# Layer norm's inverse root from one table set, the first loads in another order, and new task places in an attention and MLP kernel

## The chip, the cores and the metric

The kernel runs on one core of one Trainium2 chip. The time is device microseconds of that core, from the first to the last instruction of one execution with what lies around it; lower is better. Five engines work side by side, each through its own list of instructions in order: TensorE (PE; its weight loads stand as PEld), VectorE (DVE), ScalarE (ACT), GpSimd (POOL) and SyncE (SP), which here only issues DMAs. An instruction that must wait for another engine or a DMA holds up everything behind it in its own list.

## The reference

```python
q_rot, k_rot = rotate(q), rotate(k)                 # rotary embedding; 4 batches, 8 heads, 576 tokens, 64 wide
scores = matmul(q_rot, k_rot^T) / sqrt(64)
attn = exp(scores - max); attn /= attn.sum(-1) + 1e-9
x = matmul(attn, v)                                 # heads side by side: 2304 tokens x 512
mu = mean(x); var = mean((x - mu) ** 2)             # over the 512 features
xn = (x - mu) / sqrt(var + 1e-6) * g_ln
out = x + maximum(xn @ w_ch1, 0) @ w_ch2            # 512 -> 2048 -> 512
```

All tensors are float32. The two MLP weight matrices arrive as 64-bit floats and are decoded on the chip.

## The kernel before

**Tiling.** Attention goes over 16 pairs of heads. A pair has nine units of 128 query rows by 576 keys. For a unit TensorE makes the scores (L486; L499 for the tail unit), DVE takes the negated maximum of a row (L513), ACT the exponential with its sum (L520). The weights are then turned, on TensorE with copies by ACT (L580 to L604) or by DVE (L568), and multiplied with v (L654 or L680). DVE scales the result into the tile `xt` (L692 to L706).

**Blocks.** The 2304 tokens are five blocks, one of 512 and four of 448. Each passes a layer norm: a mean by a product with a constant matrix (L766), centring on DVE (L790), squares on ACT (L796), the variance by products (L780) into four strips of PSUM, the standard deviation by ACT's Sqrt (L808), its reciprocal on DVE (L811), a product that spreads it back over the partitions (L816), and the scaling by `g` (L825). The first block's MLP runs during attention (L1007). The other four run as two pairs of blocks in a scheme with seven products in place of eight (L1180), whose inputs are sums and differences of the normed blocks. These are written to DRAM as `hat` (L838) and read back (L1126). ACT rounds each input to a high part (L1088) and DVE or GpSimd subtracts it for the low part (L1095).

**Weights.** Each 512 KB piece of the weights is loaded as raw bits (L859), decoded by ACT, DVE and GpSimd (L868, L871, L874, L877, L880), split into a high and a low part (L893, L897), and kept in DRAM for the later blocks.

**Order.** Every step is a task with a function, the tasks that it needs, and the buffers that it takes and gives. The strings `PLACES` and `SIDES` hold each task's rank and, where a task may run on either of two engines, which one. A planner walks the tasks with assumed durations, and the order it finds is fixed on each engine. So a new string of ranks gives a new list on every engine.

**The start.** The first pair's keys are loaded in two halves of 288, the queries in 128 and 448. The first key half and the queries are issued by SP, the second key half by ACT. Rotating a half takes two products and a sum on DVE (L387), the last 448 query columns on GpSimd. The first scores need the first key half and the first 128 queries. TensorE multiplies an identity with itself 16 times meanwhile (`WARM`, L1310). One table set for ACT, with Exp, is loaded at the start (L358).

The names that matter below: `constants` and `constants3` (memsets, L351 to L364), `first_pair` (L366 on), `deviation`, `inverse` and `spread` inside `layer_norm` (L806 to L816), `pair_inputs` (L1126).

Of the kernel before, what the change touches and what calls it, by code (L numbers as in the profile page):

```python
# [64 lines left out]
WARM = 16  # L65
# [200 lines left out]
def rope_attention_then_ln_mlp(  # L266
# [477 lines left out]
    def layer_norm(n):  # L744
# [65 lines left out]
        def inverse():  # L810
            DVE.reciprocal(z["std"], z["std"])  # L811
# [597 lines left out]
```

## Time and profile before

| what | us |
|---|---|
| median of 3 runs (670.94 to 672.25) | 671.86 |
| the profiled execution | 673.72 |
| its span, first to last instruction | 671.8 |
| TensorE busy | 630.5 (94%) |
| VectorE busy | 552.2 (82%) |
| ScalarE busy | 358.5 (53%) |
| GpSimd busy | 297.6 (44%) |

The chain of work that ended last lies on TensorE for 64% of the span, on VectorE for 16%, on DMA for 8% and on ScalarE for 6%. A busy share is a mean over stages with different limits, so the rows below are read stage by stage. Line numbers are those of the kernel before. In the changed kernel L387 is L390, L486 is L489, L808 is L811 and L812, L811 is L817 to L819, L816 is L824, and lines from there on are 8 higher.

### The profile page before, as it was taken

The page shows a single profiled execution, that of the slowest core. Times are in us where ns is not written, and L with a number is a line of the kernel's source. Part 1 is how long each engine was busy: PE and PEld are TensorE (multiplying, and loading weights), DVE is VectorE, ACT ScalarE, POOL GpSimd, SP SyncE. Part 2 cuts the span into 40 slices and gives each one's busy share as a digit, 9 for nine tenths or more (in the row PEclk, how much of TensorE's full clock was granted, in tenths as well). Part 3 has the DMA queues.
Part 4 walks back from the last instruction along what each step waited for, and adds up shares of the span by engine and source line. Part 5 has one row for each costly group of instructions (what it writes and reads, how often), then busy time and mean ns, then how long its engine had stood idle before and what let it go on. Part 6 is the DMA issues. An engine that isn't in the chain of part 4 may idle for free.

```text
span 671.8 us, 13940 instructions
## 1 busy us (share of the span) xinstructions
PE 630.5 (94%) x5268; PEld 491.4 (73%) x5268; DVE 552.2 (82%) x887; ACT 358.5 (53%) x734; POOL 297.6 (44%) x223
## 2 busy tenths in 40 slices
PE   5899988999899999898898699899999999999997
PEld 4555647766675757666576587799889999999997
DVE  4998788589899989899955789978789786857876
ACT  2898877467678876688644246342343143223230
POOL 2636663454566558477510254853324212404042
PEclk7999998999999999999999899999999999999999
DMA  8477574668669889886877688778876887766666
GB/s 273 125 243 238 182 200 151 202 232 239 218 219 266 277 278 293 263 270 233 272 236 214 203 257 285 244 271 268 293 254 210 266 267 219 218 221 211 212 208 201
DMA packets 89283, 158.42 MB, mean 236 GB/s; under 512 B 11776, under 2 KB 57344, under 8 KB 88704
## 3 DMA queue, kind: packets, MB, share of 16 engines
q1 hardware_dynamic: 88080, 156.67, 73.2%
q10 hardware_dynamic: 1136, 0.85, 0.4%
q8 instruction: 42, 0.69, 0.4%
q14 instruction: 25, 0.20, 0.1%
HBM read 117.57 MB, written 39.92 MB: 234 GB/s over the span
## 4 chain that ended last, share of the span: by engine, by line
PE 64%; DVE 16%; DMA 8%; ACT 6%; issue 4%; POOL 1%; SPq 0%; ACTq 0%; DVEq 0%; POOLq 0%
PE n L1180 34%; PE sc L1007 9%; PE sc L486 6%; PE sc L654 5%; PE sc L680 4%; DVE mx L513 3%; PE sc L580 3%; ACT pt L520 2%; DMA w<-in_w2p 2%; DMA w<-s 2%; DVE pt L568 2%; DMA s<-ws 1%; ACT pt L598 1%; PE sc L499 1%; DVE tmp L1218 1%
## 5 line engine op out<-in xcount | busy, mean ns | idle before, releaser
L1180 PE MATMUL n<-x,w 128*128 128x448 f32 x672 | 143.0, 371 | 7.9 <-ACT x L1088 2.6
L1180 PEld LDWEIGHTS n<-x,w 128*128 128x128 f32 x672 | 126.5, 189 | 22.9 <-DVE x L1095 3.4
L520 ACT ACTIVATE pt<-sc,mx 128x576 f32<-128x576 f32 x144 | 105.7, 739 | 54.9 <-DVE mx L513 54.2
L1180 PE MATMUL n<-o,w 128*128 128x448 f32 x576 | 120.8, 368 | 1.9 <-DVE acc L1276 1.3
L513 DVE TENSOR_REDUCE mx<-sc 128x1 f32<-128x576 f32 x144 | 102.8, 747 | 19.5 <-PE sc L486 16.0
L1180 PEld LDWEIGHTS n<-o,w 128*128 128x128 f32 x576 | 107.7, 188 | 13.1 <-DVE acc L1276 1.7
L1088 ACT ACTIVATE o<-tmp 128x448 fp32r<-128x448 f32 x96 | 53.3, 574 | 103.1 <-PE n L1180 39.8
L486 PE MATMUL sc<-x 64*128 64x288 f32 x512 | 93.5, 442 | 8.4 <-DVE x L387 6.4
L486 PEld LDWEIGHTS sc<-x 64*128 64x128 f32 x512 | 53.1, 192 | 35.9 <-ACT pt L520 8.4
L1095 POOL TENSOR_TENSOR o<-tmp,o 128x448 fp32r<-128x448 f32 x33 | 43.1, 1319 | 81.8 <-ACT o L1088 71.5
L877 POOL TENSOR_TENSOR fw<-fw,w 128x512 int32<-128x512 int32 x32 | 43.3, 1356 | 55.7 <-ACT w L871 27.0
L1252 DVE TENSOR_TENSOR xt<-xt,n 128x448 f32<-128x448 f32 x80 | 47.8, 613 | 9.7 <-PE n L1180 8.5
L654 PE MATMUL sc<-pt,v 128*64 128x512 f32 (+2 forms) x324 | 50.5, 417 | 0.9 <-ACT pt L520 0.9
L680 PE MATMUL sc<-pt,v 32*64 32x160 f32 (+1 forms) x2016 | 43.7, 301 | 5.6 <-issue 2.1
L654 PEld LDWEIGHTS sc<-pt,v 128*64 128x64 f32 (+1 forms) x324 | 22.4, 142 | 33.7 <-issue 29.7
L680 PEld LDWEIGHTS sc<-pt,v 32*64 32x64 f32 x2016 | 36.7, 135 | 12.6 <-issue 6.6
L568 DVE STREAM_TRANSPOSE pt<-pt 128x1152 f32<-128x1152 f32 (+1 forms) x35 | 43.1, 1241 | 3.3 <-ACT pt L520 3.3
L1007 PE MATMUL sc<-xh,w 128*128 128x512 f32 x128 | 44.7, 410 | 0.7 <-ACT pt L520 0.7
L1007 PE MATMUL sc<-hh,w 128*128 128x512 f32 x128 | 44.3, 405 | 0.4 <-issue 0.4
L580 PE MATMUL sc<-ident,pt 128*128 128x128 f32 x288 | 38.1, 278 | 5.9 <-ACT pt L520 4.6
L1218 DVE SCALAR_TENSOR_TENSOR tmp<-tmp 128x448 f32<-128x448 f32 x48 | 40.6, 854 | 3.3 <-ACT tmp L1225 2.9
L580 PEld LDWEIGHTS sc<-ident,pt 128*128 128x128 f32 x288 | 31.3, 141 | 13.2 <-ACT pt L520 9.1
(129 smaller groups left out, 1062.2 us busy)
## 6 DMA issues: line engine op xcount, KB each, us to landing
w<-s SPq DMA_DIRECT2D x64, 512.0 KB
w<-v SPq DMA_DIRECT2D x96, 256.0 KB
s<-ws SPq DMA_DIRECT2D x24, 512.0 KB
v<-in_vp SPq DMA_DIRECT2D x37, 320.0 KB
x<-in_qk SPq DMA_DIRECT2D x30, 288.0 KB
xs<-in_qk SPq DMA_DIRECT2D x30, 288.0 KB
w<-in_w1p SPq DMA_DIRECT2D x16, 512.0 KB
w<-in_w2p SPq DMA_DIRECT2D x16, 512.0 KB
```

Of the source, the lines that this page charges most:

```text
L486: PE.matmul(ps[:, a, :HS], lhsT=q[r, c * P : (c + 1) * P], rhs=k[r, KEYS[a]], start=True, stop=True)
L513: DVE.tensor_reduce(out=mx, in_=st["ps", i, n][:, :, :HS], axis=AX.XY, op=ALU.max, negate=True)
L520: ACT.activation(out=halves(p), in_=st.pop(("ps", i, n))[:, :, :HS], func=AF.Exp, bias=st.pop(("mx", i, n)), scale=1.0, accum_out=total)
L568: DVE.transpose(p, p)
L580: PE.transpose(two[:, j, k * P : (k + 1) * P], p[:, at : at + P], ident)
L654: yield lambda o=o, x=x: PE.matmul(o, lhsT=w, rhs=x, start=start, stop=stop)
L680: PE.matmul(tiles[a // 2][j * D : (j + 1) * D, a % 2, x0 : x0 + (u1 - u0) * BLK], lhsT=v[r, of, k * P + j * D : k * P + (j + 1) * D], rhs= ...
L1007: PE.matmul(ps, lhsT=wt, rhs=x, start=c + m == 0, stop=c + m == NC + 1)
L1088: ACT.activation(out=o[0], in_=x(), func=AF.Relu if relu else AF.Copy)
L1180: PE.matmul(ps, lhsT=wt, rhs=x, start=fresh and kc + z == 0, stop=kc + z == 3, skip_group_check=True)
L1218: return lambda: DVE.scalar_tensor_tensor(out=out(), in0=x(), scalar=0.0, in1=y(), op0=ALU.max, op1=ALU.subtract)
L1252: DVE.tensor_tensor(out=o, in0=o, in1=ps(which, h), op=ALU.add)
```

## The change

ACT's Sqrt and DVE's reciprocal become Ln, Exp with the factor -0.5, and one Newton step of three instructions on DVE that works in the variance's own PSUM strip. The table set that holds both Ln and Exp is loaded once at the start. In the first loads SP issues the cosines ahead of the keys, and each load is ranked behind the one before it. The constants' tasks have other assumed durations, the warm-up has 20 products, and all ranks and sides are new (a line of them is shown).

```diff
-WARM = 16
+WARM = 20
...
 PLACES = (
-    "AAANADAFAEAGACABAHARAVAXAUATAWAMAKAPAdAYAgAaAlAQAIAJASA1A9A)AbA4A#A,AZAcAeAoAnAqAkAvA0AzA2AuA5A7A6A!A+A/A>A<A@A=A]A}A~BBA3A$A8A(A%A.BHBOBMBS",
+    "AAAFAHABAEAGACADAIAPAOASAQATAXAUAVAWAeAYAhAZAnARAJAKANA8AqA*AaAzA&A,AbAdAiAkAjApAmAyA1A0A3AsA2A7A6A!A+A.A=A<A>A;A]BAA_BDA5A$A9A)A%A-BKBUBHBM",
...
         for o, i in second:
             ACT.dma_start(o, i)
+        ACT.preload_act_table_set("natural_log_exp_and_others")
         ACT.activation(out=first, in_=eps_ln, func=AF.Exp)
...
-        def dma(kb, pairs, prio=-90.0):
+        def dma(kb, pairs, prio=-90.0, behind=()):
...
+            if not pairs:
+                return add({"NONE": 6.2}, go, (), prio)
...
-        l1 = dma(288, keys(KEYS[0]))
-        l2 = dma(128, queries(head))
+        l1 = dma(288, keys(KEYS[0]), behind=[l0])
+        l2 = dma(128, queries(head), behind=[l1])
...
-        l_q = dma(448, queries(rest))
+        l_q = dma(448, queries(rest), behind=[l2])
...
-            ACT.activation(out=z["std"], in_=z["var"][:, :Q], func=AF.Sqrt, bias=eps_ln, scale=1.0)
-
-        def inverse():
-            DVE.reciprocal(z["std"], z["std"])
+            ACT.activation(out=z["std"], in_=z["var"][:, :Q], func=AF.Ln, bias=eps_ln, scale=1.0)
+            ACT.activation(out=z["std"], in_=z["std"], func=AF.Exp, scale=-0.5)
+
+        def polish():
+            y = z["std"]
+            t = z["var"][:, :Q]
+            DVE.scalar_tensor_tensor(out=t, in0=t, scalar=1e-6, in1=y, op0=ALU.add, op1=ALU.mult)
+            DVE.scalar_tensor_tensor(out=t, in0=t, scalar=-0.5, in1=y, op0=ALU.mult, op1=ALU.mult)
+            DVE.scalar_tensor_tensor(out=y, in0=t, scalar=1.5, in1=y, op0=ALU.add, op1=ALU.mult)
...
-        t = add({"ACT": 1.7}, deviation, [v], N)
-        t = add({"DVE": 1.0}, inverse, [t], N)
+        t = add({"ACT": 0.75}, deviation, [v], N)
+        t = add({"DVE": 0.75}, polish, [t], N)
...
-    c1 = add({"DVE": 0.5}, constants, prio=-100.0)
-    ev["c3"] = add({"DVE": 0.9}, constants3, [c1], prio=-98.0)
+    c1 = add({"DVE": 1.3}, constants, prio=-100.0)
+    ev["c3"] = add({"DVE": 1.5}, constants3, [c1], prio=-98.0)
```

**VectorE at the start.** `x_208` and `xs_209` are the first pair's keys, `x_210` and `xs_211` its queries. Before:

```order
L387 TENSOR_TENSOR xs_209<-xs_209,rope_sb_198 128x288
L387 TENSOR_TENSOR x_208<-x_208,rope_sb_198 128x288
L361 MEMSET quarter_202 128x512
L363 MEMSET quarter_202 1x128 x4
L364 MEMSET mean_w_201 128x128
L387 TENSOR_TENSOR x_208<-x_208,xs_209 128x288
L387 TENSOR_TENSOR x_208<-x_208,rope_sb_198 128x288
L387 TENSOR_TENSOR xs_211<-xs_211,rope_sb_198 128x128
L387 TENSOR_TENSOR x_210<-x_210,rope_sb_198 128x128
L387 TENSOR_TENSOR xs_209<-xs_209,rope_sb_198 128x288
L387 TENSOR_TENSOR x_210<-x_210,xs_211 128x128
L387 TENSOR_TENSOR x_208<-x_208,xs_209 128x288
```

The same place now:

```order
L362 MEMSET quarter_202 128x512
L364 MEMSET quarter_202 1x128 x4
L365 MEMSET mean_w_201 128x128
L390 TENSOR_TENSOR xs_209<-xs_209,rope_sb_198 128x288
L390 TENSOR_TENSOR x_208<-x_208,rope_sb_198 128x288
L390 TENSOR_TENSOR x_210<-x_210,rope_sb_198 128x128
L390 TENSOR_TENSOR x_208<-x_208,xs_209 128x288
L390 TENSOR_TENSOR xs_211<-xs_211,rope_sb_198 128x128
L390 TENSOR_TENSOR x_208<-x_208,rope_sb_198 128x288
L390 TENSOR_TENSOR xs_209<-xs_209,rope_sb_198 128x288
L390 TENSOR_TENSOR x_208<-x_208,xs_209 128x288
L390 TENSOR_TENSOR x_210<-x_210,xs_211 128x128
```

The memsets moved ahead of the tensor operations. Before, the three operations on the second key half (ACT's loads) came first; now those on the first half do, and the sum of the queries is last.

**ScalarE and TensorE at the first block's layer norm.** `sq` are the squares, `std` the deviation, `xh` the normed block's high part, `fw` and `w64` weights in decoding. ScalarE before:

```order
L808 ACT_TABLE_LOAD
L808 ACTIVATE std_1133<-sc3_111,eps_ln_203 128x128
L868 ACTIVATE fw_885<-w64_1062 128x512
L598 COPY pt_1084<-sc2_110 128x2x512
L520 ACT_TABLE_LOAD
L520 ACTIVATE pt_1084,total1_207<-sc0_108,mx_1143 128x576
L831 CAST xh_1208<-xc_1082 128x512 x2
```

ScalarE now:

```order
L523 ACTIVATE pt_1097,total1_207<-sc1_109,mx_1150 128x576
L811 ACTIVATE std_1185<-sc0_108,eps_ln_203 128x128
L812 ACTIVATE std_1185<-std_1185 128x128
L876 ACTIVATE fw_884<-w64_1086 128x512
L879 ACTIVATE w64_1086<-w64_1086 128x512
L839 CAST xh_1288<-xc_1084 128x512 x4
```

Both table loads are gone; in the whole list 8 became 1, the one at the start. TensorE at this place before, to the first product with v:

```order
L780 MATMUL sc3_111<-sq_1092,mean_w_201 32x128 x4
L780 MATMUL sc3_111<-sq_1101,mean_w_201 32x128 x4
L780 MATMUL sc3_111<-sq_1110,mean_w_201 32x128 x4
L780 MATMUL sc3_111<-sq_1119,mean_w_201 32x128 x4
L486 MATMUL sc0_108<-x_745,x_892 128x288
L486 MATMUL sc1_109<-x_745,x_892 128x288
L486 MATMUL sc0_108<-x_745,x_892 128x288
L486 MATMUL sc1_109<-x_745,x_892 128x288
L580 MATMUL sc2_110<-ident_200,pt_1084 128x128 x8
L816 MATMUL sc3_111<-std_1133,quarter_202 128x128 x4
L680 MATMUL sc2_110<-pt_984,v_1042 64x160
```

TensorE now:

```order
L783 MATMUL sc0_108<-sq_1094,mean_w_201 32x128 x4
L783 MATMUL sc0_108<-sq_1106,mean_w_201 32x128 x4
L489 MATMUL sc2_110<-x_750,x_898 128x288
L489 MATMUL sc1_109<-x_750,x_898 128x288
L489 MATMUL sc2_110<-x_750,x_898 128x288
L489 MATMUL sc1_109<-x_750,x_898 128x288
L583 MATMUL sc3_111<-ident_200,pt_1097 128x128 x8
L783 MATMUL sc0_108<-sq_1117,mean_w_201 32x128 x4
L783 MATMUL sc0_108<-sq_1140,mean_w_201 32x128 x4
L683 MATMUL sc2_110<-pt_989,v_1047 64x160
```

The variance's products are split by a scores group and a turn, and 72 products with v (L683) stand between the last of them and the spread (L824).

**SyncE's queue where the paired blocks begin.** `hat` are the normed blocks in DRAM, `inv` the inverse sums of a pair of heads. Before, behind the 14th pair's `inv` reads:

```order
L1126 DMA xc_3931<-hat1_194 128x448
L1126 DMA sq_3933<-hat1_194 128x448
L1126 DMA xc_3931<-hat2_195 128x448
L1126 DMA sq_3963<-hat2_195 128x448
L1126 DMA xc_3931<-hat2_195 128x448
L1126 DMA sq_3975<-hat2_195 128x448
L1126 DMA xc_3931<-hat1_194 128x448
L1053 DMA out_0<-xt0_574 128x512
L460 DMA v_4041<-in_vp 128x640
```

Now, up to the first of the weights that follow:

```order
L1061 DMA out_0<-xt0_615 128x512
L1134 DMA sq_4251<-hat1_194 128x448
L639 DMA inv_4253<-sums15_127 64x4x128
L640 DMA inv_4253<-sums15_127 64x64
L1134 DMA xc_4122<-hat2_195 128x448
L1134 DMA sq_4314<-hat2_195 128x448
L1061 DMA out_0<-xt0_615 128x512
L1134 DMA xc_4122<-hat2_195 128x448
L1134 DMA sq_4342<-hat2_195 128x448
L1134 DMA xc_4122<-hat1_194 128x448
L1134 DMA acc_4369<-hat1_194 128x448
L923 DMA w_4371<-s006_130 128x1024
```

Six of the eight `hat` reads moved behind the last pair's `inv` reads, some behind a store as well, and the weights `s006` behind all of them; before, these weights were asked for ahead of those `inv` reads.

## Rows read from the trace of the kernel before

**Rows 1.** The page's TensorE line of 40 equal slices.
```profile
PE   5899988999899999898898699899999999999997
```

**Rows 2.** Stretches: busy us of each engine, granted clock, DMA share, GB/s.
```profile
9.40:19.60 10.20, 5.81 (x22) 3.71 (x23) 7.83 (x14) 4.21 (x9) 4.46 (x5) 0.50 0.76 267
20.00:40.00 20.00, 17.26 (x118) 10.86 (x116) 19.25 (x28) 18.30 (x41) 9.72 (x8) 1.00 0.56 169
620.00:640.00 20.00, 20.00 (x100) 18.36 (x99) 16.05 (x27) 5.00 (x10) 3.52 (x4) 1.00 0.69 212
```

**Rows 3.** Waits of TensorE: waiter, releaser, us in total, times, longest.
```profile
PE sc L486 <- DVE x L387: 6.4, 1, 6.4
...
PE sc L816 <- DVE std L811: 1.9, 2, 1.1
PE sc L780 <- DVE xc L790: 1.4, 2, 0.9
```

**Rows 4.** Timeline 0 to 30: start, us, instruction, idle before, releaser.
```profile
6.96 0.46 DVE L387 TENSOR_TENSOR xs<-xs,rope_sb 128x288 f32<-128x288 f32 x1 [5.87 <-DMA x<-in_qk]
7.34 0.45 DVE L387 TENSOR_TENSOR x<-x,rope_sb 128x288 f32<-128x288 f32 x1
...
7.84 0.48 DVE L361 MEMSET quarter<- 128x512 f32 x1
...
9.33 0.17 DVE L364 MEMSET mean_w<- 128x128 f32 x1
...
10.23 1.27 POOL L387 TENSOR_TENSOR x<-x,rope_sb 128x448 f32<-128x448 f32 x1 [0.39 <-DVE x L387]
10.44 1.21 DVE L387 TENSOR_TENSOR xs<-xs,rope_sb 128x128 f32<-128x128 f32 x1
11.27 0.67 ACT L868 ACTIVATE fw<-w 128x512 f32<-128x512 f32 x1 [7.24 <-DMA w<-in_w1p]
11.57 0.28 DVE L387 TENSOR_TENSOR x<-x,rope_sb 128x128 f32<-128x128 f32 x1
...
13.79 6.61 PE L486 MATMUL sc<-x 64*128 64x288 f32 x24 [6.42 <-DVE x L387]
...
16.90 0.74 ACT L520 ACTIVATE pt<-sc,mx 128x576 f32<-128x576 f32 x1 [3.39 <-DVE mx L513]
```

**Rows 5.** Groups on ScalarE: line, operation, tiles, count, busy us, mean ns.
```profile
L808 ACT ACT_TABLE_LOAD x4 | 5.1, 1283 | 0.1
...
L520 ACT ACT_TABLE_LOAD x3 | 3.8, 1283 | 0.1
...
L808 ACT ACTIVATE std<-sc,eps_ln 128x112 f32<-128x112 f32 (+1 forms) x5 | 1.8, 356 | 0.2
```

**Rows 6.** Groups on VectorE, shapes kept apart.
```profile
L811 DVE RECIPROCAL std<-std 128x112 f32<-128x112 f32 x4 | 3.4, 848 | 0.6 <-ACT std L808 0.5
...
L692 DVE TENSOR_TENSOR xt<-sc,inv 128x128 f32<-128x128 f32 x1 | 0.3, 292 | 3.0 <-PE sc L654 3.0
```

**Rows 7.** Timeline 98 to 116, at the first block's layer norm.
```profile
102.80 1.28 ACT L808 ACT_TABLE_LOAD   x1
...
104.09 0.37 ACT L808 ACTIVATE std<-sc,eps_ln 128x128 f32<-128x128 f32 x1
...
105.93 1.28 ACT L520 ACT_TABLE_LOAD   x1
...
108.11 5.16 PE L680 MATMUL sc<-pt,v 32*64 32x128 f32 x184 [0.83 <-ACT pt L520]
```

**Rows 8.** Timeline 300 to 330, at the third block's layer norm.
```profile
322.24 0.74 ACT L520 ACTIVATE pt<-sc,mx 128x576 f32<-128x576 f32 x1 [4.67 <-DVE mx L513]
```

**Rows 9.** Timeline 350 to 384, where the paired blocks begin, all engines but SyncE.
```profile
363.47 0.56 ACT L1088 ACTIVATE x<-xc 128x448 fp32r<-128x448 f32 x1
...
381.13 0.52 PE L1180 MATMUL n<-x,w 128*128 128x448 f32 x1 [2.59 <-ACT x L1088]
```

**Rows 10.** Timeline 336 to 384 of SyncE's queue.
```profile
370.36 0.61 SPq L637 DMA_DIRECT2D inv<-sums  x1
```

More of the change, by code (lines that the diff above doesn't have):

```diff
@@ new lines @@
+    "DpDdDjDqDxDmDuDvD0DnDrDtD$D9D-D?D{D|B,C1ClDBCyC-C:DMC3C]C?DeDYDwDzD2D_DyD1D5D4D6D3D8D#D&D.D(D/D<D@D]D^EAECEBEHD~EGELEJETD!D=EfEmEjEcEtEwE!Ev",
+    "EyE2E$E*E.E{E~E_EPEWEZEYEgEeEhEoErEuFLFVFaFYFcFdFlFoFzF2EiEqE8E:FiFuF<F_F7F+F.F>F5F#F%F]GMGaGkGqGvDbD>D7EEEFE4EnE[EKEsEzE^FjF$F6F[GpF?F~GCGB",
+    "GLGGGNGRGTGXGVGbGeGhGjGgGlGnGtG3G4G$G(G&G,GWGcG1HAG=G[G]G{HTHWHhHnHsH2H5H!H$H[G?G|HCHHHMHcHjHpHoHrHxH3H6H4H8H)H<H?H/H^HQHYH9H*H%H-IrIzI2I6Ix",
+    "I8H}IJINIeI&I[JAJHJLFnF;F8GrG#HIHPHUHNH7HwH]H;IQIIIcJGH{ICIEIDIHIOIUIYIWIdIfIlIpIoItI!I)I-I?I_I<I|I~I^JFI7I3I/I}JDJJJmJrJ-J:J@KHKNKSKZKfKiKj",
@@ new lines @@
+    "JEJNJRJPJUJOJTJZJcJeJ0J7J$J#J(KQKUKaKYKcJvJzJnJwKAKIKoKuKkKnKdKqK3K6K8K?K)K/LKLfLhH>I9ISI>I]JyJ2J^JQKvKrKyKTK@LHLYLVKsKxK0KzK7K9K.K;K,K>K[K}",
+    "LDLCLFLQLXLaLZLdLgLnLrLtLzK%L)LcLyL^L-L<L[MJMCMFMKMQMYMeMlMmMjL1L!L%L9L(L+L?L_MAMLMSMbMfMdMhMqMxM0M4M8L/L@MkMpMnMrM*M:M?NAM~NDM}NFNINaNHNUNo",
+    "NzN1KpK<LeLvLmMaL]MiLxM3MRNJM7NONCNVNuM9M.M=M<M_NENKNMNPNSNRNWNbNZNdNfNpNsNrNwNyN6N#N9N)NBNeNiN_OEN&N*N-OUOKOOOSOXOcOkOsOtO4N(N:N=N<N[N{OCOF",
+    "OGOLOrOwOzOyO2OxO1O5O3O9OZOWPCO|O7O)PFPJPYPSPWPbPfPiPlPqPrM#N7OPOVN5OMOdOqOAOYOnPVO0O:PTPZPpO6O$O,O*O/O&O.O;O=O?O<O[O{O^O}PDPIPMPLPQPdPgPjPh",
@@ new lines @@
+    "PoO@O~PNPaPBPEPnPuPUPXPtPzPkPmPsP7P5P$P,P>P@P:PvP4P6P3P8P!P&P*P+P.P;P[P{P_P}P]P|QBQAQDP-QLQCQIP)QFQGQKQSQOQQQUQYQbQeQiQkC7DoD}EIEMEQESEbEREV",
+    "EXEaEdEkElEpExE1E5E9E%E)E#E(E-E&E,E;E+E/E=E@ALAcAfAgAlAtAwA:BSAMArAuAvA4A#A^BNBTAxA/A}A?BBBLBkB4D:A(BbBgBiBlBtB1B!EUB&B-CSCeB.B]CECWCaCgC0C%",
+    "C)DEDJD;EDDNBOBmBvBrByB$FAFOFRBwB;CJCGCNCQFEFGFTB<CUCZCsCvC(FNFQFWCbCuCwC{C|DGFgFkFqFpFsFyF4FrFvF0F(F-F=GFGKGPGfGmG0G~GsC,DRDTDUDWDiF@F|GDDQ",
+    "D%D)D*D,D[F^F}GEDlD+EOE6E7E>GJGQGUENE0E3FUFXF&GOGSGZGYGdGiG7G}HFHKHgHqHuH&H+H.IBIGIRInIKE]GuGwGyG2G.G;G@HmF,GzG6G!G%G:HkH#IVG<HOHVHXHaHfHvH0",
@@ new lines @@
+    "IXHDHbHdHeHiHtHzH1IqH(H,H_IAImIvI1I;I{JBJXJbJiJ*J/J~KWJ>HlIMIbIiIkIsI$I(I:HyIPIgI0I4I%I*I.J!IwI=I@JIJSJWJlJ+J{I+JCJMJaJhJqJ6J&KKJ<J}KDK5KVKe",
+    "KmK+K-K=LILPLULkLoL5MELwJ1J?J]KOKRKbKhKlKtJ4J|KBKPKXK2K~LNLqKgK4K#K$K(K^LOLTMZK*K]K_K{LBLGLRL0McL8L$L~MGMDMMMUMuMzM5M@M^M|NQNTNlN2NXLAL2L7L&",
+    "L*L}MHMsMvLJL4L,L.L;MIMPMWN$MBMTMXMgMoM!M+M;ObMVM6M$M%M)M>M]M{OfOhO8M(NYNgNcNkNvN/OHPwNNNhNmNnNqNxOmPRPyN!OROiO!O%PAPGPKP1OJOeO#O>O]PcPxP0P#",
+    "P%P^QlE<E?E}FHFJE|FBFDFFFKFCFIFMFPFbFSFZFfFeFhFmFtFxF1FwF3F9F*F!F)F:F/F{GAGIGHGoGxG5G8G*G9G)G/G>G_G-G^HEHGHLHBHJHRHSHZH:H@H|ILH~IFIuIaITIZIy",
@@ L129 @@
[L129 to L131 removed]
+    "00000000000000000000000000011100100000000000000000000000000000000000000000000000000000000000000000000000000000000000000000001010110011000100",
@@ L132 @@
+    "01000000001001000000000000000000000000000000000000000000000000000000000000000000000000000000000000001000001000000001001001000001000000000000",
+    "0000000000000000000000000000000000000010000010000000000000000000000000000",
 )
@@ L378, in go @@
                     SP.dma_start(o, i)
-            return add({"SP": kb / RATE + (1.8 if prio < -90 else 0.0)}, go, (), prio, parts=(max(1, len(pairs)), 0.45))
+            if not pairs:
+                return add({"NONE": 6.2}, go, (), prio)
+            return add({"SP": kb / RATE + (1.8 if prio < -90 else 0.0)}, go, (), prio, parts=(len(pairs), 0.45), behind=behind)
         def rotate(x, r, loads, prio, e, dur):
```

89 lines of the change are left out of this document (35 added, 54 removed).

## The prediction, made before the result was known

> **What bounds the kernel now.** I read the page's slices first. TensorE stands at 8 or 9 tenths in most of them, at 9 in nearly all of the second half, and clearly lower only at the ends, around slice 7 and around slice 22 [rows 1]. Late in the kernel TensorE is full: 100 matmuls fill 20.00 us, 0.20 us apart, while VectorE has 16.05 [rows 2]. Nothing can be won there by shifting other engines. What can be won is TensorE's idle time before that, so I read the waits next. One wait is far larger than any other: 6.4 us before the first scores, for VectorE's rotation [rows 3]. At the layer norms TensorE waits 1.9 us in two pieces for the reciprocal and 1.4 us in two pieces for the centring [rows 3]. Between 20 and 40 us VectorE is busy 19.25 of 20 us and ScalarE 18.30, TensorE 17.26 [rows 2]: there the softmax chain sets the pace, and a head start in that chain should pass through.
>
> **The start.** VectorE's first tensor operation starts at 6.96, when its loads are in. Its second starts 0.38 later, so a 288-column operation costs 0.38 behind another and 0.45 alone; a 128-column one takes 0.28 [rows 4]. Nine such operations, six wide and three narrow, are 6 x 0.38 + 3 x 0.21 = 2.9 us, or 6 x 0.45 + 3 x 0.28 = 3.5 without any overlap (0.21 is 0.28 less the same 0.07). Before, the nine run from 6.96 to 13.79, 6.8 us. Two things fill the rest. The memsets lie in the middle, from 7.84 to 9.50 [rows 4]. And GpSimd's operations hold up VectorE's: a narrow operation at 10.44 took 1.21 in place of 0.28 and ended at 11.65, right behind GpSimd's from 10.23 to 11.50 [rows 4]. The new list does the memsets while the loads are still under way, which hides their 1.6 us. And GpSimd's second operation waits for the sum of the second key half, which now is VectorE's last but one, so only GpSimd's first can hold VectorE up: once 0.93 (1.21 - 0.28), and not two or three times.
>
> The loads are the same bytes, with the wanted half asked for first. Their arrival is bounded by 6.96 from above; from below I allow 6.0, an estimate: the operations that now lead need loads at the head of the queues, but half of what lands before them still belongs to others. With 6.5 the last operation ends at 6.5 + 2.9 + 0.93 = 10.3; the bounds are 6.0 + 2.9 = 8.9 and 6.96 + 3.5 + 0.93 = 11.4. TensorE's first scores so come near 10.3 and not at 13.79.
>
> What is late next? VectorE's first decoding step now stands ahead of the first maximum, and it needs ScalarE's conversion of the first weights, which ended at 11.27 + 0.67 = 11.94 [rows 4]. With about 0.4 for that step and 0.76 for the maximum the first exponential starts near 13.1; it was 16.90 [rows 4], so 3.8 us earlier. From 9.40 to 19.60 TensorE had the lower of its two clocks, a granted 0.50 [rows 2], after its idle stretch. If it has that again, the scores end 2.3 us behind 10.3, still near the 12.4 at which the maximum could begin; with 11.4 they end at 13.7 and 1.3 us are lost. I take **-3.5 us**, between -2.4 and -3.8 at that point. Carried through 20 to 60 us none of it must be lost for that sum; if the weight loads behind the first ones now end the waits, half or more may go.
>
> **The table loads.** Eight loads of 1283 ns become one, seven are 9.0 us of ScalarE's time [rows 5]; the eighth, at the start, stays. Five Exp are added. Their nearest row is the Sqrt on the same tile, 356 ns in the mean [rows 5], so ScalarE gains about 9.0 - 1.8 = 7.2 us. VectorE loses the reciprocal of 848 ns and gets three steps that read PSUM on 112 or 128 columns; the nearest row, 128 columns from PSUM, takes 292 [rows 6], so three are 0.88, a zero sum. Per layer norm the way from variance to spread falls from 1.28 + 0.37 + 0.85 = 2.5 us to 0.37 + 0.37 + 0.88 = 1.6. ScalarE is not the bound, so the gain is only what TensorE waits at these places.
>
> The trace shows no cost of a switch beyond the load itself: loaded from 102.80 to 104.08, the Sqrt runs from 104.09 [rows 7]. The Trainium skill (ScalarE: Activation LUTs, "What ACT_TABLE_LOAD costs") counts another 1.38 us of drain per switch, 2.66 in all. By it seven switches would be 18.6 us of ScalarE's time, not 9.0. Here the row decides, and the sum goes by it. By that page the way would fall by 1.38 us more, and the third block below could give back 5.3 us and not 2.6; a median of 659.5, which gets no share because 104.08 and 104.09 leave no room for a drain.
>
> *First block, near 100 us.* TensorE idles 1.4 us for the centring (between the variance products), 1.1 for the reciprocal (the longer of its two waits) and 0.83 ahead of the products with v [rows 3, 7], 3.3 in all. The new list puts scores and a turn between the two halves of the variance products, and 72 products with v ahead of the spread. At 184 records in 5.16 us [rows 7], two records to a product, those are 4.0 us of work over a way of 1.6. The 1.1 should go, and part of the rest. I take **-2.0**, bounds -3.3 and 0.
>
> *Second block.* TensorE shows no wait of this kind there: 0.
>
> *Third block.* The loads take 2 x 1.28 us from a ScalarE that soon after idles 4.67 us for a maximum [rows 8]. That idle time absorbs most of what is given back: **-0.5**, bounds -2.6 and 0.
>
> *Fourth and fifth.* The other wait for the reciprocal, 0.8 us, (1.9 - 1.1), is the fourth block's [rows 3]. The way becomes shorter, but in the new list 12 products stand between variance and spread where there were 18 and 24: at 0.20 apart [rows 2] the cover falls from 3.6 and 4.8 us to 2.4. A way of 1.6 and one or two VectorE operations ahead of it just fit. I take **0**, bounds -0.8 and +1.6.
>
> **The paired blocks' inputs.** Before, seven of the eight `hat` reads were asked for long before ScalarE first used one, at 363.47. Now six stand behind the last `inv` reads, the last of which went out at 370.36 to 370.97 [rows 10]. Their 6 x 224 KB and the 512 KB of weights behind them, 1.9 MB, take 8.9 us at the 213 GB/s of a full stretch [rows 2] and would be in by 379.9. TensorE's second group of products started at 381.13, after a wait of 2.59 [rows 9]. Its conversions must still come between, so this is close; in that place VectorE has one operation less ahead of the second group. I take **0**, bounds -0.5 and +6.
>
> **The other places.** The amount of work is the same on every engine, and all lists are reshuffled: each small wait now in the trace may go and others may come. **0**, bounds -2 and +2.
>
> **Sum.** -3.5 - 2.0 - 0.5 = -6.0 on the profiled execution: 673.72 - 6.0 = 667.7. That execution lies 1.86 above the median of the runs, 671.86, so I expect a median of **665.9**.
>
> **Rivals.**
> - *More goes.* The start gives 3.8, the first layer norm its whole 3.3, the third 2.6: -9.7, so 662.2. For it speaks that the waits at these places hang on the very steps that are shortened; against, that the third's ScalarE has idle time anyway.
> - *The head start is given back.* The softmax chain waits later for decoded weights, whose loads come no faster, so that by 60 us the 3.5 are gone: 669.4. VectorE's 19.25 of 20 us speak against long waits there; the DMA share of 0.56 [rows 2] says that bandwidth is free, not that the loads are asked for in time.
> - *No change.* New waits in the reshuffled lists take about what the old ones give: 671.9. It needs some 6 us of new idle time on TensorE.
> - *Slower.* The `hat` reads and the weights behind them come too late, and TensorE stands still at the head of the paired blocks. With the whole 8.9 us of these loads on its path the sum is -6.0 + 8.9 = +2.9, a median near 674.8. It decides from the point where they land some 6 us later than the second group would otherwise start, that is near 381 on the old time scale; against it stands that DMA can run ahead in that stretch, and that the second group waited for ScalarE and not for DMA [rows 9].
> - *The change doesn't do what it says:* a table load that stays between Ln and Exp. The list holds one load in all, so I give it no share of its own.
>
> **How the numbers follow.** Forecast 0.45, its own range 664 to 668; more goes 0.18; given back 0.20; no change 0.08; slower 0.09. A measurement of this kernel tells about 0.2%, 1.3 us, from no change: faster is below 670.5, slower above 673.2. So faster 0.83, same 0.08, slower 0.09. The range for 8 in 10 holds the forecast, the given-back case and most of the larger gain: 661.0 to 670.8.
>
> **What would show it.** Right: the first scores between 9 and 11.5, the first exponential near 13; one table load on ScalarE; no TensorE wait for the layer norm's DVE steps near 95 to 105; the matmuls of the paired blocks as close as before. Wrong: first scores in time but the same unit at 60 us no earlier; a TensorE wait of several us for `hat` or `s006` at the first paired products; new waits at the fourth and fifth spread, L824, on the Newton step.

## The result, and the profile after

The changed kernel takes 662.03 us in the median of 4 runs (660.44 to 663.35); the kernel before took 671.40 beside it (668.53 to 672.25, 4 runs). The ratio is 0.986, 95% interval 0.983 to 0.989: 9.4 us less. That is 3.9 below the forecast of 665.9, inside the range for 8 in 10, but outside the forecast's own 664 to 668: it is where "more goes" stood with 0.18. The profiled executions went from 673.72 to 662.65 (span 660.8), 11.1 us less.

The page's slices of the changed kernel, as in [rows 1]; the second line is TensorE's granted clock in tenths:

```profile
PE   7799988999999999998999599999999999999997
...
PEclk9799999999999999999999799999999999999999
```

The first slice rose from 5 to 7, the second fell from 8 to 7, slices 6 and 7 stayed at 8, and five slices between 11 and 26 rose from 8 to 9. The one hole, slice 23 where the paired blocks begin, went from 6 to 5. The clock is low in it and in the second slice.

The same stretches as [rows 2]:

```profile
9.40:19.60 10.20, 5.13 (x28) 3.05 (x29) 8.47 (x12) 5.99 (x14) 6.61 (x6) 0.89 0.85 314
20.00:40.00 20.00, 18.73 (x129) 12.60 (x127) 15.68 (x27) 18.20 (x40) 8.47 (x6) 0.89 0.52 166
620.00:640.00 20.00, 20.00 (x98) 18.19 (x98) 14.74 (x27) 5.28 (x10) 4.84 (x4) 1.00 0.68 211
```

TensorE is as full late in the kernel as before. Between 20 and 40 us it is busy 18.73 and not 17.26, but at a granted clock of 0.89 and not 1.00, so this is not all gain.

TensorE's waits, as in [rows 3]; the last two columns are how many and the longest:

```profile
PE n L1188 <- ACT x L1096: 5.4, 1, 5.4
PE sc L683 <- issue: 4.3, 5, 1.4
...
PE sc L489 <- DVE x L390: 1.5, 1, 1.5
PE sc L783 <- POOL sq L786: 1.5, 1, 1.5
...
PE sc L683 <- ACT pt L601: 1.2, 1, 1.2
...
PE sc L783 <- DVE xc L793: 0.6, 1, 0.6
...
PE sc L824 <- DVE std L819: 0.2, 1, 0.2
```

The 6.4 for the rotation is 1.5, the 1.9 at the spread is 0.2, the 1.4 for the centring is 0.6. What now stands on top is the head of the paired blocks, and a wait for nothing that the profile names ("issue"). Two waits are new at the norms: 1.23 us at the first, for ScalarE's copies, and 1.50 at the third (at 304.67), for GpSimd's sum of the squares.

The timeline of the start, answering [rows 4]:

```profile
6.45 0.46 DVE L390 TENSOR_TENSOR xs<-xs,rope_sb 128x288 f32<-128x288 f32 x1 [3.65 <-DMA xs<-in_qk]
...
10.34 1.24 PE L489 MATMUL sc<-x 64*128 64x288 f32 x8 [1.51 <-DVE x L390]
...
13.50 0.74 ACT L523 ACTIVATE pt<-sc,mx 128x576 f32<-128x576 f32 x1 [1.16 <-DVE mx L516]
...
18.90 5.38 PE L583 MATMUL sc<-ident,pt 128*128 128x128 f32 x24 [2.57 <-ACT pt L523]
```

Groups of instructions on ScalarE, answering [rows 5]:

```profile
L811 ACT ACTIVATE std<-sc,eps_ln 128x112 f32<-128x112 f32 x4 | 1.4, 350 | 4.4 <-PE sc L783 4.4
L358 ACT ACT_TABLE_LOAD x1 | 1.3, 1283 | 2.5 <-issue 2.5
L812 ACT ACTIVATE std<-std 128x112 f32<-128x112 f32 x4 | 1.2, 298 | 0.1
```

And on VectorE, answering [rows 6]:

```profile
L818 DVE SCALAR_TENSOR_TENSOR sc<-sc,std 128x112 f32<-128x112 f32 x4 | 1.1, 282 | 0.1
L819 DVE SCALAR_TENSOR_TENSOR std<-sc,std 128x112 f32<-128x112 f32 x4 | 1.1, 274 | 0.1
L817 DVE SCALAR_TENSOR_TENSOR sc<-sc,std 128x112 f32<-128x112 f32 x4 | 1.1, 271 | 0.0
```

One table load is left, and a Newton step takes 0.28, near the 0.29 assumed. ScalarE's busy time went from 358.5 to 350.8: 7.7 less, 7.2 forecast.

The first block's layer norm, answering [rows 7]:

```profile
104.30 2.81 PE L683 MATMUL sc<-pt,v 32*64 32x160 f32 x144 [1.23 <-ACT pt L601]
...
105.61 0.36 ACT L811 ACTIVATE std<-sc,eps_ln 128x128 f32<-128x128 f32 x1
...
106.00 0.31 ACT L812 ACTIVATE std<-std 128x128 f32<-128x128 f32 x1
...
107.36 1.16 PE L824 MATMUL sc<-std,quarter 128*128 128x128 f32 x8 [0.24 <-DVE std L819]
```

From ScalarE's start on the variance to the spread it is 1.7 us, and the products with v cover all but 0.24 of it. TensorE waits 1.23 us ahead of these products.

ScalarE behind the third block's norm, answering [rows 8]:

```profile
314.83 0.74 ACT L523 ACTIVATE pt<-sc,mx 128x576 f32<-128x576 f32 x1 [2.38 <-DVE mx L516]
```

Without its loads ScalarE still waits there for maxima, now 2.38 us.

The head of the paired blocks, answering [rows 9] and [rows 10]:

```profile
363.96 3.00 SPq L1134 DMA_DIRECT2D xc<-hat  x1
...
365.93 0.44 PE L1188 MATMUL n<-x,w 128*128 128x448 f32 x1 [1.17 <-DMA xc<-hat]
...
369.93 0.58 ACT L1096 ACTIVATE x<-xc 128x448 fp32r<-128x448 f32 x1 [6.26 <-DMA xc<-hat]
...
374.70 3.71 PE L1188 MATMUL n<-x,w 128*128 128x448 f32 x8 [5.43 <-ACT x L1096]
```

The `hat` read issued at 363.96 lets ScalarE convert only at 369.93, and TensorE's second group waits 5.43 where it waited 2.59.

### The profile page after: what moved, and what is told of

Its sections match the earlier page's. It is cut to its first block, busy times and chain, and to the rows that moved or that the text cites. A ratio compares the mean times of both kernels' runs of the same rounds, so it can differ in the third digit from the quotient of the medians.

```text
span 660.8 us, 13977 instructions
## 1 busy us (share of the span) xinstructions
PE 624.5 (95%) x5276; PEld 490.8 (74%) x5276; DVE 535.8 (81%) x890; ACT 350.8 (53%) x732; POOL 303.2 (46%) x230
## 4 chain that ended last, share of the span: by engine, by line
PE 72%; DMA 9%; DVE 8%; ACT 6%; issue 2%; POOL 2%; SPq 1%; DVEq 0%; POOLq 0%; ACTq 0%
PE n L1188 37%; PE sc L1015 12%; PE sc L489 8%; PE sc L657 7%; PE sc L583 4%; ACT pt L523 4%; PE sc L683 3%; DMA s<-ws 2%; DVE mx L516 2%; DMA hat<-xc 1%; DVE pt L571 1%; DVE xc L833 1%; DMA v<-in_vp 1%; DMA inv<-sums 1%; DMA xs<-in_qk 1%
## 5 line engine op out<-in xcount | busy, mean ns | idle before, releaser
L489 PE MATMUL sc<-x 64*128 64x288 f32 x512 | 87.3, 430 | 7.6 <-ACT pt L523 2.0
L489 PEld LDWEIGHTS sc<-x 64*128 64x128 f32 x512 | 50.0, 186 | 32.2 <-ACT pt L523 7.7
L885 POOL TENSOR_TENSOR fw<-fw,w 128x512 int32<-128x512 int32 x32 | 41.9, 1310 | 49.8 <-ACT w L879 19.4
L1103 POOL TENSOR_TENSOR o<-tmp,o 128x448 fp32r<-128x448 f32 x27 | 34.5, 1288 | 59.2 <-ACT o L1096 59.2
L683 PE MATMUL sc<-pt,v 32*64 32x160 f32 (+1 forms) x2016 | 40.8, 293 | 5.5 <-issue 4.3
L683 PEld LDWEIGHTS sc<-pt,v 32*64 32x64 f32 x2016 | 34.7, 130 | 11.3 <-issue 9.4
L583 PEld LDWEIGHTS sc<-ident,pt 128*128 128x128 f32 x288 | 33.9, 148 | 10.2 <-ACT pt L523 5.3
L1247 POOL TENSOR_TENSOR tmp<-tmp 128x448 f32<-128x448 f32 x8 | 11.0, 1376 | 64.9 <-DVE tmp L1226 57.2
```

Source lines behind the costliest of these rows:

```text
L489: PE.matmul(ps[:, a, :HS], lhsT=q[r, c * P : (c + 1) * P], rhs=k[r, KEYS[a]], start=True, stop=True)
L583: PE.transpose(two[:, j, k * P : (k + 1) * P], p[:, at : at + P], ident)
L683: PE.matmul(tiles[a // 2][j * D : (j + 1) * D, a % 2, x0 : x0 + (u1 - u0) * BLK], lhsT=v[r, of, k * P + j * D : k * P + (j + 1) * D], rhs= ...
L885: POOL.tensor_tensor(out=z["f"], in0=z["f"], in1=z["c"], op=ALU.add)
```

## The experiments

Changes below are the interval's middle times 670 us. A profile shows one execution, which lies up to 6.5 us from the median of its runs here: readings of single waits are taken from profiles, gains from medians. The first three runs each do one part of the change.

**1. The tables alone.** The kernel before with Ln, Exp and the Newton step; same order.

```diff
+        ACT.preload_act_table_set("natural_log_exp_and_others")
...
-            ACT.activation(out=z["std"], in_=z["var"][:, :Q], func=AF.Sqrt, bias=eps_ln, scale=1.0)
+            ACT.activation(out=z["std"], in_=z["var"][:, :Q], func=AF.Ln, bias=eps_ln, scale=1.0)
+            ACT.activation(out=z["std"], in_=z["std"], func=AF.Exp, scale=-0.5)
```

> The kernel before with Ln, Exp and three Newton steps in place of Sqrt and reciprocal, and nothing else; old order on every engine. Theory A, the shorter way from variance to spread makes the gain at the layer norms: the waits of TensorE at the first norm (0.89 and 1.13 us) and at the fourth and fifth (0.98, 0.80 and some of the 1.32, 0.92 and 0.94 us) shrink in the old order too, the time falls by 4 to 7 us, to 664 to 667. Theory B, the gain at the norms comes from the new order around them and the tables only make ScalarE idle more: 0.5 to 2 us, 669 to 671.

Measured 668.77, ratio 0.9974 (0.9953 to 0.9996): 1.75 us. TensorE's wait for the reciprocal at the first norm (1.13) and the one ahead of the products with v (0.83) are gone; the two for the centring stay:

```profile
PE sc L781 <- DVE xc L791: 1.4, 2, 0.9
```

So the shorter way is real without any moved task, but the size is theory B's: in the old order the tables are worth some 1.75 us (0.3 to 3.1 by the interval).

**2. The order alone.** The changed kernel with Sqrt and reciprocal.

```diff
-            ACT.activation(out=z["std"], in_=z["var"][:, :Q], func=AF.Ln, bias=eps_ln, scale=1.0)
-            ACT.activation(out=z["std"], in_=z["std"], func=AF.Exp, scale=-0.5)
+            ACT.activation(out=z["std"], in_=z["var"][:, :Q], func=AF.Sqrt, bias=eps_ln, scale=1.0)
```

> The changed kernel with Sqrt and the reciprocal back (and the table loads they bring), all else as changed, the new order included. Theory A: the norms lose what the shorter way gave, 4 to 7 us, so 666 to 669, with waits for the reciprocal ahead of the spread again. Theory B: the new order hides the long way too, 662 to 664.5, with at most a short wait at the fourth and fifth norm, where only 12 products stand between variance and spread.

Measured 665.95, 0.9941 (0.9914 to 0.9969): 4.0 us. Its timeline at the first block's norm, and its waits at the spread of all norms:

```profile
108.01 1.28 ACT L810 ACT_TABLE_LOAD   x1
...
109.31 0.37 ACT L810 ACTIVATE std<-sc,eps_ln 128x128 f32<-128x128 f32 x1
...
109.70 0.95 DVE L813 RECIPROCAL std<-std 128x128 f32<-128x128 f32 x1 [2.22 <-ACT std L810]
...
110.71 1.16 PE L818 MATMUL sc<-std,quarter 128*128 128x128 f32 x8 [1.32 <-DVE std L813]
```

```profile
PE sc L818 <- DVE std L813: 2.7, 3, 1.3
```

The new order's cover does not fit the old way of 2.7 us: 1.32 of it shows here, 2.7 us over three norms (0.2 in the changed kernel). This is theory A, at its lower edge. By the medians the tables are worth 1.75 in the old order and 5.4 in the new (9.4 - 4.0), of which these waits explain 2.5. The two differ by 3.7 us, with bounds of some 3 by the intervals: the parts do not simply add up, but by how much is not well known.

**3. The start alone.** The kernel before with the new first loads, 20 warm-up products and only the first tasks in the new order.

```diff
+HEADS = {
+    "SP": (3, 4, 5, 8, 25, 862, 871, 26, 23, 30),
...
+}
...
+    for e, first in HEADS.items():
+        for n, k in enumerate(first):
...
+            tasks[k].prio = n - 100
```

> The kernel before with the new start alone: the first loads, the 20 opening matmuls and the first tasks of SyncE (10), VectorE (24), ScalarE (21) and GpSimd (9) in the new order, everything behind them in the old one. First scores near 10.3 and first exponential near 13.5 by both theories. Theory A, the head start lasts and what was given back by 95 us was the new order's doing: 3 to 3.5 us at 95 us and in the end, 668 to 668.5. Theory B, the head start is given back in any order, as TensorE waits for the first weights of the exponentials and drops to its lower clock: 0.5 to 1.5 us at 95 us, 670 to 671.

Measured 666.66, 0.9949 (0.9928 to 0.9969): 3.4 us, more than the 668 to 668.5 of theory A. The first exponential starts at 13.48. The 43rd of them starts at 92.54 in place of 95.22, so 2.7 us lasted to the first norm in this execution.

**4. The inputs early.** The changed kernel with the `hat` reads back in front.

```diff
+    hats = [t for t in tasks if t.name.startswith("hl0.")]
+    hats[7].prio = hats[1].prio
+    for n, t in enumerate(hats[1:7]):
+        t.prio = hats[0].prio + 0.1 * (n + 1)
```

> The changed kernel with six of the eight hat reads moved up right behind the first, ahead of the last sums and inv reads, and the eighth to the second's place. Theory A, the late reads make the 1.17 and 5.43 us that TensorE waits at the head of the paired blocks: these fall to some 2 to 4 us in all, and the time by 2.5 to 4.5, to 657.5 to 659.5. Theory B, ScalarE's conversions or the tiles they take are what is late, as before the change (1.58 and 2.59 us): the wait stays within 1 us and so does the time, 661 to 663.

Measured 667.84, 0.9963 (0.9935 to 0.9991), slower than the changed kernel. TensorE's timeline there (of an execution of 674.34, 6.5 above the median, with other stretches at the lower clock):

```profile
364.70 0.49 PE L687 MATMUL sc<-pt,v 32*64 32x128 f32 x4 [2.13 <-DMA v<-in_vp]
...
385.26 6.97 PE L1192 MATMUL n<-x,w 128*128 128x448 f32 x19 [1.82 <-ACT x L1100]
```

The wait at the head fell from 5.43 to 1.82, but the last values v came late (2.13 here, 3.9 with two smaller waits). A read moved forward in a queue moves others back: neither theory had that.

**5. The changed kernel again,** beside the later ones.

> The changed kernel once more, as the measure for the runs beside it. The start alone gave 3.4 us and the tables alone 1.75 in the old order, the new order with the old tables 4.0. Theory A, the parts add up and the four runs of 662.0 are the rest of it: 661 to 663. Theory B, start and tables are all there is (3.4 + 1.75) and those four runs lay low: 664.5 to 666.

Measured 661.25 (657.00 to 663.28, 6 runs), 0.986 (0.9829 to 0.9891). The gain above the forecast is no accident of four runs.

**6. Start and tables,** the third kernel with the first one's edit: all parts of the sum that had a size, in the old order.

> The kernel before with the new start and with Ln, Exp and Newton steps, everything behind the start in the old order. Theory A, the new order behind the start is worth nothing by itself and the two parts add up: 3.4 + 1.75 = 5.2 us, 665 to 666, and no slower than the changed kernel beside it by more than 1.5 us. Theory B, the shorter way pays in full only where the new order puts other products between variance and spread: 3 us or more slower than the changed kernel beside it.

Measured 665.19, 0.9917 (0.9893 to 0.9942): 5.6 us, where 3.4 and 1.75 make 5.2 and the forecast's sum was 6.0. Its interval just does not meet the changed kernel's. So some 3.8 us (1.2 to 6.4 by the intervals) come from the new order behind the start, as theory B had it.

**7. No idle stretch at the start.** In the changed kernel TensorE stood still from 16.34 to 18.90, and a stretch at the lower clock began in it, at 17.39. Products that nobody uses fill the gaps.

```diff
-WARM = 20
+WARM = 28
...
+                fill(6, 0)
...
+            if i == 0 and c == 0:
+                fill(16, 2)
```

> The changed kernel with idle TensorE time at the start filled by products of the identity that nobody reads: 28 opening ones in place of 20, 6 ahead of the scores of the second key half, 16 ahead of the first turn (where it idled 1.51, 0.98 and 2.57 us). Theory A, the lower clock of 17.4 to 24.2 us follows from those idle stretches and costs the 24 transposes and what hangs on them: the granted clock stays at 1.00 up to 30 us, the exponentials near 35 us come 2 to 3 us earlier and the time falls by 1.5 to 3. Theory B, the softmax chain on VectorE and ScalarE sets the pace there and TensorE's clock is hidden behind it: clock higher, exponentials near 35 us and the time within 0.7 us of the changed kernel beside it.

Measured 669.38, 0.9979 (0.9961 to 0.9996), 8 us slower than the changed kernel. The stretch 12 to 30 us of this kernel (columns as in [rows 2]),

```profile
12.00:30.00 18.00, 16.37 (x126) 11.97 (x126) 14.93 (x21) 13.97 (x30) 10.92 (x8) 1.00 0.54 191
```

and in the second profile of the changed kernel:

```profile
12.00:30.00 18.00, 14.78 (x74) 10.43 (x72) 14.33 (x21) 13.74 (x30) 9.57 (x8) 0.64 0.52 185
```

The clock came as wanted, 1.00 against 0.64. The time was lost later; the waits of this kernel's TensorE:

```profile
PE sc L690 <- issue: 11.5, 10, 2.2
```

and two of them in its timeline:

```profile
266.87 1.03 PE L690 MATMUL sc<-pt,v 32*64 32x128 f32 x35 [1.91 <-issue]
...
273.06 0.52 PE L690 MATMUL sc<-pt,v 32*64 32x160 f32 x11 [2.23 <-issue]
```

The changed kernel has 4.0 to 4.3 us of these, the kernel before 2.1. Up to 255 us this kernel's exponentials are level with the second profile's, at 304 us they are 3.4 late, and the two waits shown lie between. They stand inside dense rows of products with v, where no other engine is waited for. Both theories missed them; the ninth and tenth run follow them.

**8. The inputs behind v.** The `hat` reads behind the last v loads, ahead of the sums and `inv`.

```diff
+    front = next(t for t in tasks if t.name == "store0.1")
+    hats[7].prio = hats[1].prio
+    for n, t in enumerate(hats[1:7]):
+        t.prio = front.prio + 0.1 * (n + 1)
```

> The changed kernel with six hat reads behind the last v loads and ahead of the last sums and inv reads; the eighth in the second's place. With them ahead of the v loads TensorE waited 3.9 us for v and 3.4 us at the head of the paired blocks (7.0 before that move). Theory A, the reads are the late part there and in this place nothing else waits for them: some 2 to 4 us at the head of the paired blocks, no wait for v, 2.5 to 4 us less than the changed kernel beside it. Theory B, VectorE's evacuations and ScalarE's conversions end the wait as soon as the reads don't: at most 1 us gained.

Measured 665.03 (659.14 to 666.26), 0.9895 (0.9861 to 0.9929). TensorE's timeline at the head:

```profile
365.15 5.32 PE L1193 MATMUL n<-x,w 128*128 128x448 f32 x12 [3.60 <-DVE xt L714]
...
371.42 6.82 PE L1193 MATMUL n<-x,w 128*128 128x448 f32 x23 [0.95 <-ACT x L1101]
```

The second group's 5.43 became 0.95. But VectorE now waits for `inv`, and TensorE 3.60 behind it:

```profile
364.02 0.62 DVE L709 TENSOR_TENSOR xt<-sc,inv 128x64 f32<-128x64 f32 x3 [5.18 <-DMA inv<-sums]
```

This profile is of the fastest of the six executions. In the median there is no gain, which is theory B's time; that `inv` ends the wait neither theory had.

**9. A pure shift.** The changed kernel with 30 narrow products in the opening, 60 records of TensorE, to see whether the "issue" waits go by the place in the program.

```diff
+        for k in range(30):
+            PE.matmul(ps[:, k % 4, :32], lhsT=ident, rhs=ident[:, :32], start=True, stop=True)
```

> The changed kernel with 30 more opening products, of 32 columns each, that nobody reads; the trace shows two matmuls for each such product, so every later matmul stands 60 places further on in TensorE's program, as in the run that filled the idle time. There TensorE waited 11.5 us with no releaser inside the products with v (4.0 in the changed kernel), each time at the same matmul numbers (2515, 3023, 3405 and others 128 apart) and until 1.2 to 1.5 us after a 16 KB packet of the instruction queue landed. Theory A, it is the place in the program that decides where these waits fall: again 9 to 12 us of them, 667 to 669. Theory B, the filling products themselves did the harm (clock, PSUM, VectorE's late maximum), and the waits were something else: 4 to 5 us of them, 661 to 663.

Measured 673.88, 1.0059 (1.003 to 1.0088): theory A, and worse. TensorE's waits:

```profile
PE sc L683 <- issue: 9.2, 8, 2.3
```

and its opening:

```profile
7.75 8.94 PE L1320 MATMUL sc<-ident 128*128 128x32 f32 x60
...
16.62 6.40 PE L489 MATMUL sc<-x 64*128 64x288 f32 x24
```

The shift more than doubled the "issue" waits. Not all of the 13 us is theirs. The 60 records took 8.94 and held up the first scores, of which 1.2 us against the changed kernel's second profile was left at 95 us and nothing at 255. Behind that come the waits, and new stretches at the lower clock, 3.4 us each, at 268 and 316 us.

**10. No idle stretch, same number of products.** As the seventh, but with few wide products, so that the warm-up has 20 as before.

```diff
-WARM = 20
+WARM = 13
...
+                fill(1, 0, 0, 3 * P)
...
+                fill(3, 2, HS, 224)
...
+        fill(3, 0, 0, 4 * P)
```

> The changed kernel with the idle time at the start filled as in the other such run, but by fewer and wider products, so that their number stays 20 in all and every later matmul keeps its place in the program: 13 opening ones of 128 columns and 3 of 512, 1 of 384 ahead of the scores of the second key half, 3 of 224 ahead of the first turn. Theory A, place in the program was the harm there: waits without releaser as in the changed kernel (4 to 5 us), granted clock 1.00 from 12 to 30 us, exponentials near 35 us 1 to 2 us earlier, and the time 1 to 3 us under the changed kernel's 661.3. Theory B, filling harms by itself: 665 or more. Theory C, the clock there is hidden behind the softmax chain: within 0.7 us of 661.3.

Measured 662.11 (659.12 to 667.50), 0.9887 (0.9847 to 0.9926): the changed kernel's time. Its waits:

```profile
PE sc L690 <- issue: 5.9, 5, 1.9
```

With the count kept, 11.5 became 5.9 and the loss of the seventh run went. The clock of 12 to 30 us was 0.92 and put the exponentials of 25 to 47 us 1.7 us earlier, but another low stretch at 48.9 took that back. So the time is theory C's and its mechanism is not: the exponentials did follow the clock. Of filling by itself (theory B) there is no harm.

**11. Inputs and conversions.** As the eighth, with the `inv` reads ahead of a store and eight VectorE conversions ahead of the last evacuations; the last `hat` read here stays behind the others.

```diff
+    named["rr15"].prio = named["w32"].prio + 0.1
+    for n, k in enumerate(CONVERT):
+        tasks[k].prio = tasks[LAST_OUT].prio - 0.9 + 0.1 * n
```

> The changed kernel with six hat reads behind the last v loads, the last inv reads ahead of one store, and eight of VectorE's conversions and differences of the paired inputs ahead of the last evacuations of the products with v (for these to be in order, one empty task that waits for all attention no longer stands ahead of the closing of the old buffers). With the reads alone moved, VectorE stood idle 5.18 us for inv while the reads were in, TensorE 3.60 and 0.95. Theory A, VectorE's order is what is left of that wait: 1 to 3 us at the head of the paired blocks (6.1 to 7.0 in the changed kernel), 658 to 660. Theory B, inv ends the wait there whatever stands ahead of it: 3.5 us or more, 661 to 663.

Measured 663.83 (658.37 to 664.71), 0.9894 (0.9857 to 0.993). TensorE's timeline at the head, and VectorE's first evacuation behind its conversions:

```profile
368.11 2.69 PE L1199 MATMUL n<-x,w 128*128 128x448 f32 x12 [3.36 <-DMA acc<-hat]
...
371.43 0.47 PE L1199 MATMUL n<-x,w 128*128 128x448 f32 x1 [0.64 <-ACT x L1107]
...
366.97 0.62 DVE L715 TENSOR_TENSOR xt<-sc,inv 128x64 f32<-128x64 f32 x3 [0.65 <-DMA inv<-sums]
```

Waits of 4.3 remain (with one more of 0.26), of 6.1 to 7.0 in the changed kernel's two profiles: nearer theory B, though the profile names the last `hat` read, not `inv`, for the longest. The time is no better than the changed kernel's 661 to 662. No version here beats it.

**12. The new order up to the third norm,** start and tables as changed, the old order behind: to place the 3.8 us.

```diff
-HEADS = {
...
-        t = add({"ACT": 1.7}, deviation, [v], N)
-        t = add({"DVE": 1.0}, polish, [t], N)
+        t = add({"ACT": 0.75}, deviation, [v], N)
+        t = add({"DVE": 0.75}, polish, [t], N)
```

Against the sixth kernel the ranks are new for the first 184 tasks of TensorE, 307 of VectorE, 267 of ScalarE, 105 of GpSimd and 127 of SyncE; behind them the old order stands.

> The changed kernel with the new order up to the first sum of the third layer norm (184 of TensorE's tasks, 307 of VectorE's, 267 of ScalarE's, 105 of GpSimd's, 127 of SyncE's) and the old order behind it, the hat reads early with it. Start and tables in the old order gave 665.2, the whole new order 661.3. Theory A, the new order pays at the first norm, where products with v now stand between variance and spread, and its late hat reads take back 1 to 2 us: 659.5 to 661.5. Theory B, it pays behind the third norm (the fourth and fifth norm and the head of the paired blocks): 664 to 666.

Measured 667.57, 0.9953 (0.9927 to 0.9979): 3.1 us, no more than start and tables alone (5.6), and slower than either theory had. The new order's gain lies behind the third norm's first sum, or needs the whole list; up to there it brings nothing that lasts. What the seam between the two orders costs by itself is not told apart.

## Why the prediction was right, and where its sizes were off

- **The start (-3.5): right.** First scores at 10.34 (10.3 forecast), first exponential 13.50 (13.1), 3.40 earlier. Alone it is worth 3.4 in the median. Whether it lasts was a rival, and single profiles do not settle it. At the 43rd exponential the third and sixth run's kernels are 2.7 and 2.9 us ahead of the kernel before, the changed one only 0.8 (94.40 against 95.22). But the eighth run's, whose list is the same up to there, is 4.9 ahead (90.28), and what it lacks is the changed kernel's 6.8 us at the lower clock near the start. So "given back" is not shown for the new order. One new wait in its list is plain; it does not stand in the third run's:

```profile
50.19 1.00 PE L489 MATMUL sc<-x 64*128 64x288 f32 x6 [1.27 <-DVE xt L695]
```

- **The tables (no drain): right.** Here the second run adds [rows 7] again: a load from 108.01 to 109.29, the next function at 109.31. The Trainium skill (ScalarE: Activation LUTs, "What ACT_TABLE_LOAD costs") has 2.66 us for the switch; the measurement decides for 1.28.
- **First norm (-2.0): near.** From the 43rd to the 55th exponential it took 49.0 us before and 46.95 with the tables alone, each with 3.4 us at the lower clock in it. The third run, with the old tables and the old order there and no such stretch, took 47.4; the two profiles of the changed kernel, without one too, 45.78 and 45.5. So some 1.6 us of the 49.0 are clock, and the change gave 1.6 to 1.9. The waits that went are those named, but not all: of 3.3 us before, 2.1 are left (0.58, 1.23 and 0.24), with the 1.23 new. The cover was priced too high: the 5.16 us of [rows 7] had a granted clock of 0.67, and the 72 products now take 2.81 us, not 4.0. It was just enough.
- **Third, fourth and fifth norm (-0.5, 0): near nothing, as forecast.** At the third the 1.50 for GpSimd's sum is new, against 0.35 for VectorE's before. The spread's 0.8 at the fourth norm went. The changed kernel's waits of the fourth and fifth are 0.64 in all; the third run, with old tables and old order, shows 0.6 too, so what the profile of before had more than that belongs to its execution.
- **The paired inputs (0, bounds -0.5 and +6): the mechanism of the slower rival, at a small price.** TensorE's waits at the head sum to 7.0 and 6.1 in the two profiles of the changed kernel, 5.0 before and 3.8 in the third run: 1 to 3 us are lost there, not 8.9. With these reads further ahead in SyncE's queue another load ended a wait: v in the fourth run, `inv` in the eighth; in the eleventh the profile names the last `hat` read itself.
- **Other places (0, bounds -2 and +2): the term that was mis-sized.** Start and tables gave 5.6 of the forecast 6.0; the whole gave 9.4. The 3.8 us between are the new order behind the start, net of what the paired inputs lose, and the bound of 2 was too narrow. Without the tables the order adds only 0.6 to the start (second against third run), which points to a gain that needs the short way; the intervals leave that open. "More goes" came out at 662.2, the right time for another reason, which is luck: neither the third norm nor the start gave more than forecast.
- **Slips that change nothing:** slice 7 of [rows 1] is no lower than eight others, the low one is slice 23; the full stretch of [rows 2] has 212 GB/s, not 213; and the median with a drain at every switch, put at 659.5, comes to 659.7.
- **Still open:** what in the new order saves the time. Where is narrower. Counted by TensorE's matmuls, the changed kernel's second profile is level with the twelfth run's within 0.13 us from 240 to 264 us, and 3.3 ahead at 350. The 1176 matmuls from the 2404th to the 3579th, in each kernel the same kinds and numbers and all at the full clock, take 87.1 and 86.1 us in the changed kernel's two profiles, 87.6, 87.1 and 86.6 in the eighth, tenth and eleventh run, but 88.7 to 90.5 in the third, sixth and twelfth. The first two of these have the old order there, the twelfth from 279 us on (as its TensorE list shows). About two thirds of the difference are TensorE's busy time (81.1 to 81.9 against 82.8 to 83.5), not its waits: the matmuls stand closer together, and no single wait carries it. The old order up to the third norm with the new one behind was not tried.

## What to carry to other kernels

A shorter way at a synchronisation point and an order that fits it were worth more together (here 9.4) than the tables alone and the order with the new start alone add up to (1.75 + 4.0): so after shortening a latency, let the scheduler place the tasks again. A read moved in a shared queue should be priced by who gets the slot: of three ways of moving the `hat` reads ahead two made another load late, and none gained in the median. Before a kernel's opening is padded with instructions, look at the waits of the whole list: here 30 more products there came with losses of 8 and 13 us, most of them hundreds of microseconds later.

## What the runs showed of the hardware that was not expected

**Waits at fixed places of the program.** TensorE's "issue" waits, 0.2 to 2.3 us each, stand in rows of matmuls about 20 ns apart (144 in 2.81 us). Counted over all of TensorE's matmuls, nearly all of them in the changed kernel, the seventh and the ninth run fall on one grid with steps of 127 to 128: 1367, 1495, 3023 and 3405 in the changed kernel; 2515, 2643, 3023 and others in the seventh; 2515, 2643 and 3023 again in the ninth, though 60 records were put in ahead in the last two. By the trace's packet records each of these ends 1.2 to 1.6 us after a 16 KB packet of the instruction queue landed (265.35 for the wait that ended at 266.87, 271.68 for 273.06). One wait of 1.2 us is of another kind: it stands at 3602 in the changed kernel and 60 further on in the other two, and no packet landed in the 13 us ahead of it. The instruction queue on the page of the changed kernel, with packets and MB:

```profile
q8 instruction: 42, 0.69, 0.5%
```

TensorE's 5276 matmuls over 42 packets are 126 to a packet, about the step of the grid. This points to the fetch of TensorE's own program, which such dense rows outrun. What such a wait costs then hangs on which matmuls stand at those numbers: the seventh and ninth run moved them and paid, the tenth kept the count and did not. No run took the fetches away, so the cause is inferred.

**Stretches at the lower clock come and go.** The same program, up to some 340 us, had a granted clock of 0.50 (1.2 of 2.4 GHz) for 6.8 us from 17.4 in one profile, 13.7 from 11.3 in the second, and, with only the `hat` reads moved, in three stretches of 20.5 in all before 60 us. In the eighth run's profile, whose list is the same there, the start has none, and its exponentials run 4.1 us earlier than the second profile's from 27 us on. So the start's 3.5 us lie within what one execution differs from another, and only medians could weigh it.

**Narrow products are not cheap.** The ninth run's products of 32 columns, each with its own weights, stand 0.112 us apart at a granted clock of 1.00 and 0.213 at 0.50, record by record. The 128-column products of the changed kernel's opening stand 0.112 and 0.213 apart too: a quarter of the columns saved nothing here.
